# A long-convolution spectrum made one feed ahead, its halves moved by DMA, and eleven zero products at the start

## The chip, the core and the metric

The kernel runs on one core of a Trainium2 chip. The core has a matrix engine (TensorE, in the profile PE, its weight loads PEld), VectorE (DVE), ScalarE (ACT), GpSimd (POOL) and a queue engine, SyncE (SP), that only issues transfers; ACT and POOL can issue transfers too. Each engine works through its own instructions in a fixed order and waits on semaphores for the others. Working data lie in SBUF, 128 partitions wide; matmuls write to PSUM, in banks of 512 words per partition. The metric is the device time of one execution in microseconds (us), the median of several runs. Before the change it is 1204.5 us.

## The reference

Two kinds of layer alternate, A, B, A, B, over `x` of shape 2048 x 576, each behind a layer norm and added to its input:

```python
# A: Fourier mixing, both transforms as given matrices
a = x @ hid_re.T;  b = x @ hid_im.T
y = seq_re @ a - seq_im @ b
# B: gate, with a long causal convolution that does not depend on x
k_shift = causal_conv4(k, shift_k);  kv = k_shift * v
y = irfft(rfft(pad(kv)) * rfft(pad(ssm_k)))[:2048] + kv * ssm_D
out = q * y            # q is the normed x
```

The arguments `k`, `v`, `shift_k`, `ssm_k` and `ssm_D` are the same in both B layers, so the long convolution is made once. All is in float32. A float32 matmul is made of three in a rounded 32-bit format: high part by high part, high by low, low by high; that is why operands are "split" (ScalarE copies the rounded high part, VectorE subtracts to get the low part) and why matmuls come in threes.

## The kernel before

The first A layer's product with the sequence matrix runs in `layer` (line 291): four blocks of 512 output rows, two matrices (`g`), 16 steps of 128 rows each. One step is 14 matmuls of 512 columns (12 into four accumulators `s0` to `s3`, 2 into `rm`), with one 128 x 512 piece of the matrix, loaded by SP and split by `load_c` two steps ahead. In the first block each step also needs its normed block of `x` (`get_x0`, `to_x`). After each block the product with the hidden matrix (`hidden`, line 267) follows in pieces of 27 matmuls of 288 columns.

Beside it runs `branch` (line 338), a generator that makes the long convolution and is advanced between half steps of the layer. Its transforms of 4096 points are split as 128 by 16 and have three parts: first 128-point products (`f1_products`, stored to DRAM as `t`), the 16-point stage, and the last 128-point products (`i2_products`). The 16-point stage handles 64 "feeds" (`mids`: two halves of 288 channels times 32 groups of four frequencies). A feed is a 128 x 576 slice, loaded by SP (`load_feed`) and split (`split_feed`): its first 288 columns carry the signal, the next the convolution kernel. Partitions 0 to 63 (`lo`) end up with real parts, 64 to 127 (`hi`) with imaginary parts. For each feed the stage does this:

- `mid_inverse` of an older product: three matmuls, a copy out of PSUM by ACT, a store.
- `mid_kernel`: three matmuls give the kernel's spectrum in a PSUM bank; four ACT copies place it in `kk`, a buffer of two 288-column planes: plane 0 gets the real part in both halves, plane 1 the imaginary part in both halves, the lower one negated. There are two `kk` buffers.
- `mid_round`: the product of the feed before is split into `yf` for its inverse.
- `mid_signal`: three matmuls give the signal's spectrum; VectorE multiplies it with plane 0 (in place in `kk`), then each half with the other half of plane 1 into `p2`, and adds.
- the split of the feed two further on and the load of the one four further on.

The order in time comes from three things. The generator yields the planned cost of what it just issued (0.4, 1.6, 1.1 per feed; `I2_COST` for `i2_products`), and the loop over the layer's steps (line 752) advances it until the sum of these costs reaches what is due. A scheduler at build time then fixes each engine's order, roughly the written order where operands are expected in time. The helper `act` chains the branch's ACT instructions, so that these stay as written. All the narrow products, of the stage, of `hidden` and of `i2_products`, share three PSUM banks (`bank`, line 76).

At the start TensorE has nothing to do until the first loads have landed and been split.

Of the kernel before, what the change touches and what calls it, by code (L numbers as in the profile page):

```python
# [10 lines left out]
F32 = mybir.dt.float32  # L11
FR = mybir.dt.float32r
AF = mybir.ActivationFunctionType
OP = mybir.AluOpType

P = 128
S = 2048
D = 576
J = S // P
TB = 4  # L20
NT = 512
HD = D // 2
# [22 lines left out]
I2_COST = 2.0  # L45
# [13 lines left out]
SC_AT = 8 + 4 * STAT  # L59
RT_AT = SC_AT + 4 * REM + 5 * WIDE  # L60
FLT = RT_AT + NT


@with_exitstack
def fnet_h3_kernel(ctx: ExitStack, tc: tile.TileContext, x, c_mat, w_re, w_im, k_pad, v, shift_k,
                   ssm_k, ssm_d, f1c, i2c, midc, out):
    nc = tc.nc
# [5 lines left out]
    def mm(ps, lhsT, rhs, first, last, more=False):  # L73
        nc.tensor.matmul(ps, lhsT, rhs, start=first, stop=last, skip_group_check=more)  # L74
# [4 lines left out]
    acc4 = [psp.tile([P, NT], F32, tag=f"s{i}", name=f"s{i}") for i in range(4)]  # L79
# [25 lines left out]
    def flat(words, dt, name):  # L105
        return sb.tile([P, words], dt, tag=name, name=name)
# [29 lines left out]
    def two(v):  # L136
        return v.rearrange("p (a n) -> p a n", a=2)

    mats = flat(X_END + 3 * WIDE, FR, "mats")
    xs = mats[:, :X_END].rearrange("p (j n) -> p j n", j=J)  # L140
# [7 lines left out]

    flts = flat(FLT, F32, "flts")
    mhalf = flts[:, :1]  # L150
# [13 lines left out]

    nc.vector.memset(mhalf, -0.5)
    nc.scalar.activation(flts[:, 1:2], mhalf, AF.Copy)

    def norm_stats(src):
        m = ring["stat"]()
        st, mv, ve, rs = m[:, :12].rearrange("p (a c) -> p a c", a=2), m[:, 12:14], m[:, 14:15], m[:, 15:16]  # L170
        for i in range(2):
            nc.vector.bn_stats(st[:, i, :], src[:, i * HD:(i + 1) * HD])
        nc.vector.bn_aggr(mv, st)
        nc.vector.tensor_scalar(ve, mv[:, 1:2], EPS, None, op0=OP.add)  # L174
        pows.append(nc.gpsimd.tensor_tensor(rs, ve, mhalf, OP.pow).ins)  # L175
        return mv, rs, m[:, 16:17]
# [161 lines left out]
    def branch():  # L338
# [132 lines left out]
        lo, hi = slice(0, 64), slice(64, 128)  # L471

        def mid_half(df, o):
            ps = bank()
            mm(ps[:, :HD], mc[:, 0, :], df[0][:, o:o + HD], True, False)
            mm(ps[:, :HD], mc[:, 0, :], df[1][:, o:o + HD], False, False)
            mm(ps[:, :HD], mc[:, 1, :], df[0][:, o:o + HD], False, True)
            return ps
# [3 lines left out]
        def act(*args, **kw):  # L482
            if last_act:
                with tc.issue_after(last_act[-1]):
                    last_act.append(nc.scalar.activation(*args, **kw).ins)  # L485
            else:
                last_act.append(nc.scalar.activation(*args, **kw).ins)
# [4 lines left out]

        def mid_kernel(df):
            pk, kk = mid_half(df, HD), two(ring["kk"]())
            act(kk[:, 0, :], pk[:, :HD], AF.Copy)
            act(kk[lo, 1, :], kk[hi, 0, :], AF.Copy)
            act(kk[hi, 1, :], kk[hi, 0, :], AF.Copy, scale=-1.0)
            act(kk[hi, 0, :], kk[lo, 0, :], AF.Copy)
            return kk

        def mid_signal(df, kk):
            px = mid_half(df, 0)
            p1, p2 = kk[:, 0, :], ring["p2"]()
            nc.vector.tensor_tensor(p1, px[:, :HD], p1, OP.mult)
            nc.vector.tensor_tensor(p2[lo], px[hi, :HD], kk[hi, 1, :], OP.mult)
            nc.vector.tensor_tensor(p2[hi], px[lo, :HD], kk[lo, 1, :], OP.mult)
            nc.vector.tensor_tensor(p1, p1, p2, OP.add)
            return p1

        def mid_round(p1):  # L510
            yf = two(ring["yf"]())
            act_split(yf[:, 0, :], yf[:, 1, :], p1)
            return yf

        def mid_inverse(hf, qg, yf):
            pv = bank()
            mm(pv[:, :HD], mc[:, 2, :], yf[:, 0, :], True, False)
            mm(pv[:, :HD], mc[:, 2, :], yf[:, 1, :], False, False)
            mm(pv[:, :HD], mc[:, 3, :], yf[:, 0, :], False, True)
            vo = ring["vo"]()  # L520
            act(vo, pv[:, :HD], AF.Copy)
            nc.scalar.dma_start(v_d[hf][4 * qg:4 * qg + 4].rearrange("q j c d -> (q j c) d"), vo)

        def i2_products(hf, j, fc, vf):
            yo = ring["vo"]()
            ps = bank()
            for c in range(2):
                cs = slice(c * HD, (c + 1) * HD)
                mm(ps[:, :HD], fc[:, c, :], vf[0][:, cs], c == 0, False)
                mm(ps[:, :HD], fc[:, c, :], vf[1][:, cs], False, False)  # L530
                mm(ps[:, :HD], fc[:, 2 + c, :], vf[0][:, cs], False, c == 1)
            act(yo, ps[:, :HD], AF.Copy)
            nc.scalar.dma_start(yb_d[j][:, hf * HD:(hf + 1) * HD], yo)
# [3 lines left out]
        feeds = []  # L537
# [7 lines left out]
        landed, halves, fcs, yfs = {}, {}, {}, []  # L545
# [8 lines left out]
        def load_fc(k):  # L554
            if k < len(rows):
                fcs[k] = quads(ring["fc"]())
                load_fr(fcs[k], i2c[rows[k]])
# [9 lines left out]
        for i in range(2):  # L567
            split_feed(i)
            load_feed(i + 2)
            load_fc(i)  # L570
        used, ahead, product = 0, 2, None
        for i, (kind, hf, q) in enumerate(feeds):
            df = halves.pop(i)
            if kind:
                i2_products(hf, q, fcs.pop(used), df)
                load_fc(used + ahead)
                used += 1
            else:
                if len(yfs) == MID_LAG:
                    mid_inverse(*yfs.pop(0))  # L580
                    yield 0.4
                kk = mid_kernel(df)
                if product is not None:
                    yfs.append((*product[:2], mid_round(product[2])))
                yield 1.6
                product = hf, q, mid_signal(df, kk)
            split_feed(i + 2)
            load_feed(i + ahead + 2)
            if i == last_mid:
                yield 0.4  # L590
                mid_inverse(*yfs.pop(0))
                yfs.append((*product[:2], mid_round(product[2])))
                while yfs:
                    yield 0.4
                    mid_inverse(*yfs.pop(0))
                for name, t, at, words in (("fc", m1, spare, 4 * P), ("land", flts, kk_at, D)):
                    old = ring[name]
                    held = [old.tiles[(old.n + m) % 2] for m in range(2)]
                    fresh(name)
                    lay(t, at, (name, words, 2))  # L600
                    ring[name].tiles.extend(held)
                for m in range(2):
                    load_fc(used + ahead + m)
                    load_feed(i + ahead + 3 + m)
                ahead = 4
            yield I2_COST if kind else 1.1

    def sums(src, junk):
        m = ring["stat"]()
# [111 lines left out]
    used = 4  # L721
# [382 lines left out]
```

## Time and profile before

| what | value |
|---|---|
| median of 3 runs | 1204.5 us (1203.71 to 1204.72) |
| the profiled execution | 1203.45 us |
| its span, first to last instruction | 1201.7 us |
| TensorE busy | 1181.4 us (98%) |
| VectorE busy | 839.9 us (70%) |
| ScalarE busy | 666.0 us (55%) |
| moved by DMA | 261.95 MB, mean 218 GB/s |

Matmuls are pipelined and overlap, and the profile models their ends, so TensorE's 98% says that it is seldom empty, not that it works at its full rate; the distance from one start to the next tells that. A row of a group gives busy time, mean duration of one instruction, and the idle time of the engine just before such instructions with what ended most of it. A row of a stage gives its times and the busy time of each engine in it.

### The profile page before, as it was taken

To read this page: it belongs to the slowest core of one execution; us is meant where nothing else is said; L and a number is where in the kernel's file an instruction comes from. 1 tells how busy PE (TensorE), PEld (TensorE's weight loads), DVE (VectorE), ACT (ScalarE), POOL (GpSimd) and SP (SyncE) were. 2 spreads that over 40 slices of the span, in tenths; PEclk is the share of its full clock that TensorE was granted. 3 is DMA by queue.
4 is the path that set the end of the run, shared out by engine and by line. 5 is a ranking of instruction groups with operands and counts; after the bars stand their busy time and mean duration, and the time that the engine had idled before them with its cause. 6 is when DMAs were issued, how large, how long until landed. Compare 5 with 4: busy or idle time off the path is not lost.

```text
span 1201.7 us, 18251 instructions
## 1 busy us (share of the span) xinstructions
PE 1181.4 (98%) x6320; PEld 1026.7 (85%) x6320; DVE 839.9 (70%) x1498; ACT 666.0 (55%) x1335; POOL 75.3 (6%) x116
## 2 busy tenths in 40 slices
PE   7999999999999999999999999999999999999997
PEld 6888888988888888888988898888888888789997
DVE  7889983679777677675447766865776777674764
ACT  7865665679877768675435666534444445450210
POOL 2210000000000000001101121000000000001111
PEclk9999999999999999999999999999999999999999
DMA  9879898546756767648967686872772786795621
GB/s 355 273 242 310 282 296 262 177 133 182 217 183 194 212 178 207 194 143 247 308 202 237 221 257 204 278 259 71 225 274 71 216 283 213 270 339 155 218 92 40
DMA packets 146110, 261.95 MB, mean 218 GB/s; under 512 B 15841, under 2 KB 44769, under 8 KB 146018
## 3 DMA queue, kind: packets, MB, share of 16 engines
q1 hardware_dynamic: 102674, 205.58, 53.5%
q10 hardware_dynamic: 36432, 42.63, 10.2%
q0 software_dynamic: 6912, 12.59, 3.9%
q8 instruction: 49, 0.80, 0.3%
q14 instruction: 43, 0.35, 0.1%
HBM read 194.09 MB, written 66.65 MB: 217 GB/s over the span
## 4 chain that ended last, share of the span: by engine, by line
PE 84%; DVE 5%; ACT 4%; DMA 4%; issue 2%; POOL 1%; SPq 0%; ACTq 0%; POOLq 0%; DVEq 0%
PE s L74 46%; PE bk L74 33%; PE rm L74 5%; ACT flts L485 1%; DMA flts<-in_c_mat 1%; DVE mats L189 1%; DMA t<-ud 1%; DVE mats L92 1%; DVE f1f L386 1%; DMA t<-flts 1%; ACT mid L485 1%; ACT mats L91 1%; POOL flts L615 0%; DVE f1f L381 0%; DMA flts<-in_ssm_k 0%
## 5 line engine op out<-in xcount | busy, mean ns | idle before, releaser
L74 PE MATMUL s<-mats 128*128 128x512 f32 x2088 | 531.4, 392 | 1.3 <-DVE u L92 0.8
L74 PEld LDWEIGHTS s<-mats 128*128 128x128 f32 x2088 | 381.7, 188 | 71.9 <-DVE u L92 1.7
L92 DVE TENSOR_TENSOR mats<-flts,mats 128x512 fp32r<-128x512 f32 x206 | 141.1, 687 | 60.9 <-ACT mats L91 57.8
L91 ACT ACTIVATE mats<-flts 128x512 fp32r<-128x512 f32 x206 | 128.6, 628 | 81.8 <-PE bk L74 33.8
L74 PE MATMUL bk<-mid 128*128 128x288 f32 x768 | 131.2, 300 | 1.7 <-ACT flts L485 0.9
L74 PEld LDWEIGHTS bk<-mid 128*128 128x128 f32 x768 | 114.3, 188 | 21.3 <-ACT flts L485 8.4
L491 DVE TENSOR_TENSOR mid<-flts,mid 128x576 fp32r<-128x576 f32 (+1 forms) x160 | 101.9, 637 | 33.6 <-ACT mid L485 28.0
L74 PE MATMUL bk<-w,u 128*128 128x288 f32 x864 | 120.8, 296 | 0.4 <-DVE w L232 0.4
L74 PEld LDWEIGHTS bk<-w,u 128*128 128x128 f32 x864 | 117.3, 188 | 4.1 <-ACT flts L485 1.3
L485 ACT ACTIVATE flts<-bk 128x288 f32<-128x288 f32 x160 | 62.0, 405 | 86.8 <-PE bk L74 73.9
L74 PE MATMUL rm<-mats 128*128 128x512 f32 x304 | 94.9, 391 | 0.0
L485 ACT ACTIVATE mid<-flts 128x576 fp32r<-128x576 f32 (+1 forms) x159 | 86.7, 582 | 7.3 <-DMA flts<-t 3.3
L485 ACT ACTIVATE flts<-flts 64x288 f32<-64x288 f32 x192 | 85.0, 443 | 5.9 <-ACT flts L485 0.4
L431 ACT ACTIVATE flts<-bk 128x288 f32<-128x288 f32 x128 | 49.2, 409 | 47.1 <-PE bk L74 40.0
L74 PE MATMUL bk<-f1r 128*128 128x288 f32 x384 | 64.9, 301 | 7.2 <-ACT f1r L91 7.2
L74 PEld LDWEIGHTS bk<-f1r 128*128 128x128 f32 x384 | 59.8, 192 | 14.2 <-ACT f1r L91 7.6
L74 PE MATMUL bk<-mats 128*128 128x288 f32 (+1 forms) x376 | 67.8, 317 | 0.0
L74 PEld LDWEIGHTS rm<-mats 128*128 128x128 f32 x304 | 56.9, 188 | 12.1 <-DVE flts L264 0.3
L74 PE MATMUL s<-t,mats 128*128 128x512 f32 x264 | 65.5, 390 | 1.6 <-DVE t L92 1.6
L278 DVE TENSOR_TENSOR flts<-flts,bk 128x288 f32<-128x288 f32 x48 | 21.8, 453 | 63.2 <-PE bk L74 61.0
L175 POOL TENSOR_TENSOR flts<-flts 128x1 f32<-128x1 f32 x35 | 29.6, 846 | 526.0 <-DVE flts L174 522.6
L74 PEld LDWEIGHTS s<-t,mats 128*128 128x128 f32 x264 | 49.5, 188 | 12.2 <-DVE t L92 2.0
(143 smaller groups left out, 1500.7 us busy)
## 6 DMA issues: line engine op xcount, KB each, us to landing
flts<-in_c_mat SPq DMA_DIRECT2D x148, 256.0 KB, 3.7
ph<-in_c_mat SPq DMA_DIRECT2D x54, 512.0 KB, 4.4
t<-flts ACTq DMA_DIRECT2D x64, 288.0 KB, 4.5
flts<-t SPq DMA_DIRECT2D x64, 288.0 KB, 2.9
flts<-in_c_mat SPq DMA_DIRECT2D x30, 512.0 KB, 5.0
vd<-flts ACTq DMA_DIRECT2D x64, 144.0 KB, 2.3
flts<-vd SPq DMA_DIRECT2D x32, 288.0 KB, 4.9
mid<-in_i2c POOLq DMA_DIRECT2D x32, 256.0 KB, 5.6
```

Of the source, the lines that this page charges most:

```text
L74: nc.tensor.matmul(ps, lhsT, rhs, start=first, stop=last, skip_group_check=more)
L91: a = nc.scalar.activation(h, src, AF.Copy).ins
L92: return a, nc.vector.tensor_tensor(l, src, h.bitcast(F32), OP.subtract).ins
L175: pows.append(nc.gpsimd.tensor_tensor(rs, ve, mhalf, OP.pow).ins)
L189: made.append(nc.vector.tensor_tensor(t[:, D + REM:], y[:, :NC * P], h[:, :NC * P], OP.subtract).ins)
L278: added[:] = [nc.vector.tensor_tensor(r[:, cs], r[:, cs], ps[:, :HD], OP.add).ins]
L386: nc.vector.tensor_tensor(rp, rp, out_t, OP.add)
L431: stored[:] = [nc.scalar.activation(so[:, c, :], ps[:, :HD], AF.Copy).ins]
L485: last_act.append(nc.scalar.activation(*args, **kw).ins)
L491: nc.vector.tensor_tensor(l, src, h.bitcast(F32), OP.subtract)
```

## The change

Three things are edited. In `mid_kernel` ACT writes only two half copies out of PSUM, the real part to the lower and the imaginary part to the upper half of `kk`; two transfers issued by SP copy each to the other half. The negation moves from ACT's copy into one of VectorE's products, which becomes a `scalar_tensor_tensor` with a factor of -1. In the stage's loop the kernel spectrum of feed i + 1 is made within feed i, ahead of the signal products of feed i, and kept in `spectra`; the yields are cut anew to 0.4, 0.6, 0.5 and 1.6 (and 0.5 after an `i2_products` that is followed by a feed). At the start VectorE clears a part of the buffer `xs` that is not in use yet, and TensorE multiplies it with itself eleven times into `s0` to `s3`, which the layer's first step clears again.

```diff
+WARM = 11
@@ start
     nc.vector.memset(mhalf, -0.5)
     nc.scalar.activation(flts[:, 1:2], mhalf, AF.Copy)
+    warm = xs[:, J - 1, :NT + P]
+    nc.vector.memset(warm.bitcast(F32), 0.0)
+    for i in range(WARM):
+        mm(acc4[i % 4], warm[:, NT:], warm[:, :NT], True, True)
@@ branch
         def mid_kernel(df):
             pk, kk = mid_half(df, HD), two(ring["kk"]())
-            act(kk[:, 0, :], pk[:, :HD], AF.Copy)
-            act(kk[lo, 1, :], kk[hi, 0, :], AF.Copy)
-            act(kk[hi, 1, :], kk[hi, 0, :], AF.Copy, scale=-1.0)
-            act(kk[hi, 0, :], kk[lo, 0, :], AF.Copy)
+            act(kk[lo, 0, :], pk[lo, :HD], AF.Copy)
+            act(kk[hi, 1, :], pk[hi, :HD], AF.Copy)
+            nc.sync.dma_start(kk[hi, 0, :], kk[lo, 0, :])
+            nc.sync.dma_start(kk[lo, 1, :], kk[hi, 1, :])
             return kk
 
         def mid_signal(df, kk):
             px = mid_half(df, 0)
             p1, p2 = kk[:, 0, :], ring["p2"]()
             nc.vector.tensor_tensor(p1, px[:, :HD], p1, OP.mult)
-            nc.vector.tensor_tensor(p2[lo], px[hi, :HD], kk[hi, 1, :], OP.mult)
+            nc.vector.scalar_tensor_tensor(p2[lo], px[hi, :HD], -1.0, kk[hi, 1, :], op0=OP.mult, op1=OP.mult)
             nc.vector.tensor_tensor(p2[hi], px[lo, :HD], kk[lo, 1, :], OP.mult)
             nc.vector.tensor_tensor(p1, p1, p2, OP.add)
             return p1
@@ the stage's loop
-        used, ahead, product = 0, 2, None
+        used, ahead, product, spectra = 0, 2, None, {}
+
+        def kernel_ahead(i):
+            if i < len(feeds) and not feeds[i][0]:
+                spectra[i] = mid_kernel(halves[i])
+                return True
+
+        kernel_ahead(0)
         for i, (kind, hf, q) in enumerate(feeds):
             df = halves.pop(i)
             if kind:
                 i2_products(hf, q, fcs.pop(used), df)
                 load_fc(used + ahead)
                 used += 1
+                if kernel_ahead(i + 1):
+                    yield 0.5
             else:
                 if len(yfs) == MID_LAG:
                     mid_inverse(*yfs.pop(0))
                     yield 0.4
-                kk = mid_kernel(df)
                 if product is not None:
                     yfs.append((*product[:2], mid_round(product[2])))
-                yield 1.6
-                product = hf, q, mid_signal(df, kk)
+                yield 0.6
+                if kernel_ahead(i + 1):
+                    yield 0.5
+                product = hf, q, mid_signal(df, spectra.pop(i))
             split_feed(i + 2)
             load_feed(i + ahead + 2)
...
-            yield I2_COST if kind else 1.1
+            yield I2_COST if kind else 1.6
```

## The prediction

> **What bounds the kernel now.** I read the engine totals first, then the chain that ended last, then the 16-point stage by windows and by weight loads, because a busy TensorE in this profile isn't yet a TensorE at its rate.
>
> ```profile
> span 1201.7 us, 18251 instructions
> ...
> PE 1181.4 (98%) x6320; PEld 1026.7 (85%) x6320; DVE 839.9 (70%) x1498; ACT 666.0 (55%) x1335; POOL 75.3 (6%) x116
> ```
>
> The profiled execution took 1203.45 us, its span plus 1.75 us around it; the median of the runs is 1204.5, which is 1.05 more. The sum below is made against 1203.45. TensorE is the bound, so time is won or lost only where its matmuls stand further apart than they must. Their dense spacing comes from the chain in order of time:
>
> ```profile
> 654.75 2.72 PE s L74 x12
> 657.47 0.45 PE rm L74 x2
> 657.92 2.72 PE s L74 x12
> ...
> 1078.97 115.02 PE bk L74 x866
> ```
>
> From 654.75 to 657.92 lie 14 matmuls of 512 columns: 0.2264 us each. The last 866 of 288 columns take 115.02 us: 0.1328 each. The 16-point stage fills about 220 to 550 us. Its row for all engines, and its row for the tile bk alone, which holds the narrow matmuls (columns of the first: time, then busy us and count of PE, PEld, DVE, ACT, POOL, the granted clock, the busy share of the DMA engines and GB/s):
>
> ```profile
> 220.00:550.00 330.00, 327.92 (x1852) 285.47 (x1852) 247.23 (x485) 249.27 (x543) 5.30 (x10) 1.00 0.61 182
> ...
> 220.00:550.00 330.00, 168.96 (x1087) 1.00 0.61 182
> ```
>
> Of 1852 matmuls 1087 are narrow and 765 wide: 765 x 0.2264 + 1087 x 0.1328 = 173.2 + 144.4 = 317.6 us. So of 330 us TensorE loses 12.4 at full clock; that is all the stage can give. Who makes it wait is seen at the weight loads of the narrow matmuls in this window:
>
> ```profile
> L74 PEld LDWEIGHTS bk<-mid 128*128 128x128 f32 x628 | 93.8, 188 | 18.9 <-ACT flts L485 8.4 <-DVE flts L506 2.6 <-DVE mid L491 0.7
> L74 PEld LDWEIGHTS bk<-w,u 128*128 128x128 f32 x459 | 62.0, 188 | 2.1 <-ACT flts L485 1.1 <-DVE flts L506 0.4
> ```
>
> 9.5 us end with an ACT copy out of a PSUM bank (L485, flts<-bk) and 3.0 us with L506, the last of VectorE's reads of a signal's bank: TensorE waits for one of three banks to come free.
>
> **Part 1, ScalarE's copies.** Per kernel spectrum the change drops three ACT copies between halves of `kk` and splits the copy out of PSUM into two of 64 partitions.
>
> ```profile
> L485 ACT ACTIVATE flts<-flts 64x288 f32<-64x288 f32 x192 | 85.0, 443 | 5.9 <-ACT flts L485 0.4
> L485 ACT ACTIVATE flts<-bk 128x288 f32<-128x288 f32 x136 | 52.2, 404 | 55.4 <-PE bk L74 47.0 <-ACT flts L485 5.5 <-DVE mid L491 1.3
> ```
>
> Removed: 192 x 0.443 = 85.0 us. Added: one more PSUM copy for each of 64 spectra; as long per partition, so 0.404 each, 25.9 us (at most 0.443, the 64-partition row: 28.4). ACT's work in the stage falls from 249.3 to 190.2 us, 76% to 58%. A dense feed (14 wide and 9 narrow matmuls) lasts 3.17 + 1.20 = 4.37 us, and ACT gives back 0.92 of it. ACT runs this branch in written order, so the copy that frees a bank has been standing behind 1.33 us of SBUF copies. Ends: nothing (the free time lies elsewhere) and all 9.5. I take two thirds, -6.3, because the removed work stands just ahead of the late copies; a third stays for copies late behind other work (splits, rounding).
>
> **Part 2, VectorE no longer waits for the spectrum.**
>
> ```profile
> L504 DVE TENSOR_TENSOR flts<-bk,flts 128x288 f32<-128x288 f32 x64 | 29.1, 455 | 37.1 <-ACT flts L485 36.6
> ```
>
> Today the first product of a signal waits 36.6 us in all for the copies, holding the signal's bank. With the spectrum made one feed ahead it should be there. Of the 3.0 us charged to L506 I take half, -1.5 (ends 0 and -3.0). `scalar_tensor_tensor` in place of `tensor_tensor` for one product:
>
> ```profile
> L627 DVE SCALAR_TENSOR_TENSOR flts<-flts 128x576 f32<-128x576 f32 x10 | 8.1, 809 | 0.0
> ```
>
> 809 ns against 0.76 us for the two-operand form at 576 columns (L491 in the next fence) is 7%: 0.03 x 64 = 2 us on a VectorE that is 75% busy and loses 36.6 us of waiting. Cost nothing; without that cover, at most 2.
>
> **Part 3, the two transfers, and the new waits.** A spectrum now needs two SP transfers of 64 x 288, and the product for one feed must be rounded before the spectrum two feeds later may overwrite its `kk` (two of them, and the product is made in place). That is a loop over two feeds: ACT copies, transfer, products, sum, rounding, next copies. VectorE's part today:
>
> ```profile
> 307.29 0.46 DVE L504 TENSOR_TENSOR flts<-bk,flts 128x288 f32<-128x288 f32 x1 [1.23 <-ACT flts L485]
> 307.75 0.46 DVE L491 TENSOR_TENSOR mid<-flts,mid 128x288 fp32r<-128x288 f32 x1
> 308.25 0.46 DVE L505 TENSOR_TENSOR flts<-bk,flts 64x288 f32<-64x288 f32 x1
> 308.72 0.45 DVE L506 TENSOR_TENSOR flts<-bk,flts 64x288 f32<-64x288 f32 x1
> 309.20 0.76 DVE L491 TENSOR_TENSOR mid<-flts,mid 128x576 fp32r<-128x576 f32 x1
> 309.88 0.45 DVE L507 TENSOR_TENSOR flts<-flts 128x288 f32<-128x288 f32 x1
> ```
>
> First product to end of sum: 3.04 us (307.29 to 310.33), other work in between included. Two ACT copies 0.81; rounding, high part on ACT 0.44 (as long as the 64-partition copy), low part on VectorE 0.46. Together 4.75, plus the transfer from issue to landing. No row shows SBUF to SBUF; the nearest in this window:
>
> ```profile
> flts<-t SPq DMA_DIRECT2D x54, 288.0 KB, 2.9
> flts<-in_c_mat SPq DMA_DIRECT2D x54, 256.0 KB, 3.1
> vd<-flts ACTq DMA_DIRECT2D x57, 144.0 KB, 2.3
> wd<-w SPq DMA_DIRECT2D x9, 576.0 KB, 4.6
> ```
>
> The nearest is `vd`, also out of SBUF, in rows of 288 words: 2.3 us; each new transfer has half its bytes. The far end is 4.6. At 2.3 the loop takes 7.1 us against 2 x 4.37 = 8.74: it fits with 1.7 to spare, and over the stage's mean feed (330/64 = 5.16 us) with 3.3. By the last row a transfer that queues behind a big one takes the loop to 9.4.
>
> The Trainium skill, "DMA: Bandwidth & Descriptors", section "Queues, rings and completion order", says that SP's transfers share one ring on each DMA engine and are taken in ring order. By that rule a small copy issued behind a matrix load waits for its bytes, as the last case supposes; no row here shows such a pair.
>
> On SP, 128 issues are added, and behind each that still waits for ACT stand the feed loads, the matrix loads and, here and there, `wd` stores; ACT's splits wait for the loads. The code issues them two feeds and two row blocks ahead, 8.7 us at the dense rate against landings of 2.9 to 3.1, so a delay of a microsecond or two is covered. The spectrum's matmuls also move one feed up: they need the split of their feed sooner, and the two ACT copies wait in ACT's queue for VectorE's rounding, with the split and the next bank's copy behind them. I charge these new waits +3.0 together: 0.05 us a feed, a third of what ACT's late copies cost today (9.5/64 = 0.15). The planner's costs don't add to it: 0.4 + 0.6 + 0.5 + 1.6 a feed against 0.4 + 1.6 + 1.1, both 3.1; POOL's loads keep their place. Ends: 0, and 64 feeds x (9.35/2 - 4.37) = +20.
>
> **Part 4, the zero products.** They start once VectorE has cleared the operand, in time that TensorE spends waiting for its first load:
>
> ```profile
> 0.81 0.06 DVE L165 MEMSET flts<- 128x1 f32 x1 [0.81 <-PEq L1096]
> ...
> 6.96 2.60 PE L74 MATMUL bk<-f1r 128*128 128x288 f32 x9 [6.96 <-ACT f1r L91]
> 9.37 2.07 PE L74 MATMUL s<-mats 128*128 128x512 f32 x4
> ...
> 15.25 2.90 PE L74 MATMUL s<-mats 128*128 128x512 f32 x12
> ...
> 18.57 2.91 PE L74 MATMUL s<-mats 128*128 128x512 f32 x12
> ```
>
> The first nine narrow matmuls take 2.41 us, 0.268 each, half the dense rate. From 9.37 to 15.25 stand 14 wide and 6 narrow ones, 3.97 us of work in 5.88. So 1.2 + 1.9 = 3.1 us go to the slow start. Eleven wide zero products at half rate take 11 x 0.45 = 5.0 us; clearing 640 columns takes VectorE, after its first clearing, some 0.85 (0.76 for 576, above), so they start at about 1.75 and end by 6.75, ahead of 6.96: no delay. Were the clearing slower, TensorE would start later by what is over 0.2 us. But TensorE, once fast, meets its data:
>
> ```profile
> 12.00:16.00 4.00, 4.00 (x18) 3.28 (x18) 4.00 (x14) 3.71 (x7) 2.37 (x4) 1.00 1.05 389
> ...
> 14.04 0.67 ACT L186 ACTIVATE mats<-early 128x576 fp32r<-128x576 f32 x1
> ...
> 18.03 0.68 DVE L189 TENSOR_TENSOR mats<-early,mats 128x512 fp32r<-128x512 f32 x1
> ```
>
> The second row block is rounded at 14.71 and needed at 15.25: 0.54 us to gain. The third's low part is ready at 18.71 and used by the fifth matmul from 18.57, at 19.48: 0.77. VectorE, which makes these parts, has no idle time to give here (its row, third column of pairs, is 4.00 of 4.00 us), so I take -0.5; ends 0 and -3.1.
>
> The Trainium skill, "TensorE: Matmul & The Clock Gate", Part 1 on the HAM clock gate, gives half rate until one free-running window of about 3.4 us has been busy. By it 5 us of zeros hold a whole window in about half of all starts, (5.0 - 3.4)/3.4, and the term is -0.5 or 0; the trace agrees on the half rate (0.268 against 0.133), and no run here shows the phase.
>
> Sum: -6.3 - 1.5 + 3.0 - 0.5 = -5.3 us: 1198.2 for such an execution, 1199.2 beside the median.
>
> **Rivals.** (a) The transfer loop becomes the bound. For it: the loop is closed over only two buffers, DMA engines are 61% busy in the stage, and a landing of 4.6 us has a row. Against: the nearest rows have 2.3 to 3.1. It eats the gains (-8.3 with the start) when 64 x ((4.75 + L)/2 - 4.37) exceeds them, from L = 4.25 us; at 4.6 it costs 20 us, 1204.5 + 20 - 8.3 = 1216. Just past the point it gives 1207. (b) It is hidden anyway: the bank that ACT frees sooner waits for another reader, the zeros meet data that isn't there, new waits equal old ones: 1203.5. For it: VectorE is as busy as ACT and takes over. (c) Everything that ACT holds back comes, with no new wait: 9.5 and 0.8 at the start: 1204.5 - 10.3 = 1194.2. The other 12.4 - 9.5 = 2.9 belong to waits that part 1 doesn't touch. (d) The zeros give their whole 3.1 as well as the main case: 1196.6; against it stand the two gaps of 0.54 and 0.77.
>
> **How the numbers follow.** A change under 0.2% (2.4 us) can't be told from none. Main case 0.47 (its own range 1195.5 to 1202), (c) and (d) together 0.11, (b) 0.18, (a) 0.24. Faster 0.58, same 0.18, slower 0.24. The range leaves out the far half of (a) and of (c): 1194.5 to 1208.
>
> **What would show it.** Right: in the stage ACT busy falls to about 190 us, L504's wait for ACT is gone, the weight-load idle ended by L485 shrinks to about 3; the new SP transfers land in 2 to 3 us. Wrong: L504 waiting for a DMA, ACT waiting for the rounding (L491) with banks held behind it, or narrow weight loads ended by L491; at the start, the second block's matmul still near 15.2.

## The result, and the profile after

The changed kernel takes 1215.11 us (median; 1211.93 to 1216.98) beside 1204.11 for the kernel before on the same chip: ratio 1.0091, interval 1.0076 to 1.0106, so 11.0 us slower. The profiled execution took 1216.98 us, 13.5 more than the one of before; the reading below is against that.

The totals of the page after:

```profile
span 1215.1 us, 18579 instructions
...
PE 1188.9 (98%) x6331; PEld 1029.1 (85%) x6331; DVE 841.8 (69%) x1499; ACT 616.0 (51%) x1207; POOL 75.3 (6%) x116
```

ScalarE lost 50 us of work, as meant. The 16-point stage by windows, all engines and then the tile bk alone (columns as in the prediction):

```profile
220.00:550.00 330.00, 319.41 (x1774) 275.63 (x1774) 238.88 (x468) 192.42 (x400) 5.30 (x10) 0.99 0.70 203
...
220.00:550.00 330.00, 165.06 (x1036) 149.53 (x1036) 90.41 (x199) 78.81 (x193) 0.99 0.70 203
```

In the same 330 us TensorE started 1774 matmuls, not 1852. By the prediction's sum, 738 wide and 1036 narrow ones are 304.7 us of work: 25.3 us are lost where 12.4 were. These 12.9 are nearly the whole 13.5; some 1.7 of them lie in one stretch of 3.41 us at half clock (last section). The weight loads of the narrow matmuls in this window, and the waits of ScalarE and of VectorE (waiting line, line waited for, us, times, longest); L490 is before's L485, L496 its L491, L509 its L504, L512 its L507:

```profile
L75 PEld LDWEIGHTS bk<-mid 128*128 128x128 f32 x604 | 91.1, 188 | 30.4 <-DVE mid L496 8.7 <-ACT mid L490 8.5 <-ACT flts L490 3.5
```

```profile
ACT flts L490 <- DVE mid L496: 18.9, 29, 1.3
ACT mid L490 <- DVE flts L512: 18.7, 20, 4.6
```

```profile
DVE mid L496 <- ACT mid L490: 31.4, 39, 2.8
...
DVE flts L509 <- DMA flts<-flts: 9.8, 8, 5.3
```

The first row is the result in short. What ScalarE's copies out of the banks (flts L490) held back fell from 8.4 to 3.5 us, but two waits that were under 1 us now end 17.2: TensorE waits for the two parts of a feed's split (mid L490, ScalarE's high part; mid L496, VectorE's low part). And ScalarE's copies into `kk` wait 29 times for VectorE's rounding of a product, which they did not do before.

The stage's first microseconds show the whole chain. ScalarE's rows of the timeline after, then VectorE's, then TensorE's (start, us, then in brackets the idle time and who ended it):

```profile
221.22 1.70 ACT L490 ACTIVATE flts<-bk 64x288 f32<-64x288 f32 x4 [2.74 <-PE bk L75]
...
229.55 0.45 ACT L490 ACTIVATE mid<-flts 128x288 fp32r<-128x288 f32 x1 [4.63 <-DVE flts L512]
...
230.91 0.41 ACT L490 ACTIVATE flts<-bk 64x288 f32<-64x288 f32 x1 [0.92 <-DVE mid L496]
231.86 0.41 ACT L490 ACTIVATE flts<-bk 64x288 f32<-64x288 f32 x1
232.29 1.02 ACT L490 ACTIVATE mid<-flts 128x576 fp32r<-128x576 f32 x2
```

```profile
226.52 0.46 DVE L509 TENSOR_TENSOR flts<-bk,flts 128x288 f32<-128x288 f32 x1 [5.25 <-DMA flts<-flts]
226.90 0.75 DVE L496 TENSOR_TENSOR mid<-flts,mid 128x576 fp32r<-128x576 f32 x1
...
229.02 0.45 DVE L512 TENSOR_TENSOR flts<-flts 128x288 f32<-128x288 f32 x1
...
230.36 0.46 DVE L496 TENSOR_TENSOR mid<-flts,mid 128x288 fp32r<-128x288 f32 x1
```

```profile
227.70 0.54 PE L75 MATMUL bk<-mid 128*128 128x288 f32 x2 [1.60 <-DVE mid L496]
...
233.03 0.40 PE L75 MATMUL bk<-mid 128*128 128x288 f32 x1 [2.08 <-ACT mid L490]
```

Read it from the top. ScalarE copies the first two spectra at 221.22. VectorE's first product waits 5.25 us for a transfer, and the low part of the next feed stands behind it, ready only at 227.65: TensorE waits 1.60. The sum ends at 229.47, ScalarE's rounding has waited 4.63 us for it, VectorE's part of the rounding ends at 230.82, and only then may ScalarE overwrite `kk` (230.91). The split of a feed stands behind that copy, starts at 232.29, and TensorE has waited 2.08 us for it. From 211 to 277 us the changed kernel starts 22 wide and 9 narrow matmuls fewer than before: 22 x 0.2264 + 9 x 0.1328 = 6.2 us.

```profile
211.00:277.00 66.00, 64.81 (x406) 57.94 (x406) 48.51 (x95) 47.39 (x100) 0.00 (x0) 1.00 0.50 154
...
211.00:277.00 66.00, 47.69 (x321) 43.86 (x321) 18.87 (x43) 8.49 (x22) 1.00 0.50 154
```

```profile
211.00:277.00 66.00, 60.32 (x375) 54.07 (x373) 44.72 (x88) 34.28 (x70) 0.00 (x0) 0.97 0.57 165
...
211.00:277.00 66.00, 47.53 (x312) 43.96 (x312) 18.57 (x41) 13.03 (x32) 0.97 0.57 165
```

(The first pair is before, the second after.) Further on the waits are mostly shorter, but they come back. ScalarE's rows, the copies for every second spectrum, then a product of VectorE and a group of matmuls of TensorE:

```profile
303.56 0.84 ACT L490 ACTIVATE flts<-bk 64x288 f32<-64x288 f32 x2
...
313.18 0.84 ACT L490 ACTIVATE flts<-bk 64x288 f32<-64x288 f32 x2 [0.58 <-DVE mid L496]
...
323.61 0.84 ACT L490 ACTIVATE flts<-bk 64x288 f32<-64x288 f32 x2 [0.59 <-DVE mid L496]
```

```profile
319.97 0.46 DVE L509 TENSOR_TENSOR flts<-bk,flts 128x288 f32<-128x288 f32 x1 [2.50 <-PE rm L75]
```

```profile
322.23 0.53 PE L75 MATMUL bk<-mid 128*128 128x288 f32 x2 [1.54 <-DVE mid L496]
```

From one filling of a buffer to the next pass 9.62 and 10.43 us, against 8.74 for two dense feeds. That alone shows little: the first products of every second feed start 10.4 us apart in the mean of the kernel before, too (10.7 after). The waits inside say more.

In the first round the transfers land within 2.5 us. VectorE starts the product 4.06 us after the copies have ended, and the sum ends 2.57 us later. ScalarE takes the rounding up only 1.13 us after that, because a split of the layer's matrix and a copy out of a bank stand ahead of it in its order. The rounding takes 0.93 us, and the next copies have waited 0.58 us for it.

In the second round the product at 319.97 waits 2.50 us. The profile names TensorE, but the product's transfer, issued at 313.61, landed 6.26 us later, at 319.88, the longest landing of all; the low part of a split stands behind that product, and TensorE waits 1.54 us.

By the landings in the trace eight more first products start 0.1 us after their transfer has landed; with this one they have waited 7.6 us, and with the 5.25 at the entry 12.9.

At the start, TensorE's rows after, then of before:

```profile
1.62 4.27 PE L75 MATMUL s<-mats 128*128 128x512 f32 x11 [1.62 <-DVE mats L169]
6.62 1.85 PE L75 MATMUL bk<-f1r 128*128 128x288 f32 x9 [0.73 <-ACT f1r L92]
...
13.86 3.17 PE L75 MATMUL s<-mats 128*128 128x512 f32 x12
...
29.99 1.46 PE L75 MATMUL bk<-f1r 128*128 128x288 f32 x9 [1.43 <-ACT flts L436]
...
35.01 1.29 PE L75 MATMUL s<-mats 128*128 128x512 f32 x5
```

```profile
34.35 1.98 PE L74 MATMUL s<-mats 128*128 128x512 f32 x8
```

The second row block starts at 13.86, not 15.25: 1.39 us won. At 29.99 TensorE waits for a copy out of a bank, and the matmul that before started at 34.35 now starts at 35.01. A lead of 0.38 us is there again from about 150 us on, up to the stage.

### The profile page after: what moved, and what is told of

Same layout as the page of the kernel before. It is cut to its first block, busy times and chain, and to the rows that moved or that the text cites. A ratio compares the mean times of both kernels' runs of the same rounds, so it can differ in the third digit from the quotient of the medians.

```text
span 1215.1 us, 18579 instructions
## 1 busy us (share of the span) xinstructions
PE 1188.9 (98%) x6331; PEld 1029.1 (85%) x6331; DVE 841.8 (69%) x1499; ACT 616.0 (51%) x1207; POOL 75.3 (6%) x116
## 4 chain that ended last, share of the span: by engine, by line
PE 81%; DMA 6%; DVE 5%; ACT 4%; issue 2%; POOL 0%; SPq 0%; ACTq 0%; POOLq 0%; DVEq 0%
PE s L75 45%; PE bk L75 32%; PE rm L75 4%; DMA flts<-in_c_mat 1%; DMA flts<-flts 1%; ACT mid L490 1%; DVE mid L496 1%; ACT flts L490 1%; DMA t<-flts 1%; DMA early<-in_x 1%; ACT mats L92 1%; DMA flts<-t 1%; DVE f1f L391 0%; DMA t<-ud 0%; DVE mats L194 0%
## 5 line engine op out<-in xcount | busy, mean ns | idle before, releaser
L490 ACT ACTIVATE flts<-bk 64x288 f32<-64x288 f32 (+1 forms) x224 | 91.5, 408 | 126.0 <-PE bk L75 88.4
L75 PE MATMUL bk<-mid 128*128 128x288 f32 x768 | 134.8, 302 | 10.3 <-DVE mid L496 5.5
L75 PEld LDWEIGHTS bk<-mid 128*128 128x128 f32 x768 | 115.1, 188 | 33.8 <-ACT mid L490 10.5
L496 DVE TENSOR_TENSOR mid<-flts,mid 128x576 fp32r<-128x576 f32 (+1 forms) x160 | 101.6, 637 | 58.9 <-ACT mid L490 50.4
L490 ACT ACTIVATE mid<-flts 128x576 fp32r<-128x576 f32 (+1 forms) x159 | 92.0, 585 | 25.2 <-DVE flts L512 19.5
L436 ACT ACTIVATE flts<-bk 128x288 f32<-128x288 f32 x128 | 49.4, 410 | 46.2 <-PE bk L75 43.8
L75 PE MATMUL bk<-mats,t 128*128 128x288 f32 (+1 forms) x368 | 59.3, 303 | 0.0
L75 PEld LDWEIGHTS bk<-mats 128*128 128x128 f32 x376 | 55.5, 188 | 3.4
```

The costliest lines, as they stand in the source:

```text
L436: stored[:] = [nc.scalar.activation(so[:, c, :], ps[:, :HD], AF.Copy).ins]
L496: nc.vector.tensor_tensor(l, src, h.bitcast(F32), OP.subtract)
```

## The experiments

Two theories stood at first. Order: the spectrum, made a feed ahead, needs its split a feed sooner, and its copies stand ahead of that split in ScalarE's order. Transfers: their landing holds VectorE's products. Ratios are to the kernel before on the same chip, with their intervals; the changed kernel's is 1.0091 (1.0076 to 1.0106).

**Each part alone.** The kernel before with nothing but the zero products:

```diff
+    warm = xs[:, J - 1, :NT + P]
+    nc.vector.memset(warm.bitcast(F32), 0.0)
+    for i in range(WARM):
+        mm(acc4[i % 4], warm[:, NT:], warm[:, :NT], True, True)
```

> The kernel before with the zero products alone. Both theories of the stage say nothing here. From the progress of the first layer's matmuls in the changed kernel (1.38 us ahead at the second row block, 0.38 ahead from about 130 us on) I expect 0.4 us less than before, between 0 and 0.8; if it were the whole slow start it would be 3.1 less.

1202.87 us, ratio 1.0001 (0.9989 to 1.0013): nothing. The changed kernel without these four lines:

> The changed kernel without the zero products. Both theories: the loss stays whole, 10.5 to 12 us over before; if the two edits disturbed each other it would be under 8.

1210.98 us, ratio 1.0064 (1.0045 to 1.0084): 8.0 us over before, less than the 10.5 to 12 expected, but not under 8. Most of the loss is the stage's; the interval just meets that of the whole change, so whether the zero products cost something there stays open.

**Order without transfers, twice.** First the changed kernel without its two transfers (`kk` is cleared once instead):

```diff
-            nc.sync.dma_start(kk[hi, 0, :], kk[lo, 0, :])
-            nc.sync.dma_start(kk[lo, 1, :], kk[hi, 1, :])
...
+        for _ in range(2):
+            nc.vector.memset(ring["kk"](), 0.0)
```

> The changed kernel without the two transfers, so the copied halves of the spectrum stay zero (they are cleared once, some 1.2 us of VectorE) and those products are left out of the result; ACT's load, the order and everything else stay. Order theory (the spectrum's matmuls come a feed sooner than the split that they need, which stands on ACT behind copies that wait for a rounding): still 7 to 11 us over before, weight loads still waiting for splits by some 13 us. Transfer theory (VectorE waits in its order for transfers that land in up to 6.3 us, and the low part of a split stands behind that wait): 0 to 5 us under before, weight loads waiting for splits under 4 us.

1208.43 us, ratio 1.0040 (1.0026 to 1.0053), in between: the order alone costs some 5 us, and the rest needs the transfers. ScalarE's wait for the rounding is untouched:

```profile
ACT flts L490 <- DVE mid L496: 22.6, 28, 4.1
```

Then the changed kernel with ScalarE's four copies of before in their place:

```diff
-            act(kk[lo, 0, :], pk[lo, :HD], AF.Copy)
-            act(kk[hi, 1, :], pk[hi, :HD], AF.Copy)
-            nc.sync.dma_start(kk[hi, 0, :], kk[lo, 0, :])
-            nc.sync.dma_start(kk[lo, 1, :], kk[hi, 1, :])
+            act(kk[:, 0, :], pk[:, :HD], AF.Copy)
+            act(kk[lo, 1, :], kk[hi, 0, :], AF.Copy)
+            act(kk[hi, 1, :], kk[hi, 0, :], AF.Copy, scale=-1.0)
+            act(kk[hi, 0, :], kk[lo, 0, :], AF.Copy)
```

> The changed kernel with its order and zero products, but ScalarE makes the four copies of before and no transfer is issued. Order theory: ScalarE is as busy as before (about 250 us in the stage) and its copies wait for the rounding as well, so the kernel takes 1212 to 1220. Transfer theory: without a landing the spectrum is in time, and it takes 1201 to 1206.

(The negated product is a `tensor_tensor` again in this run.) 1215.83 us, ratio 1.0112 (1.0095 to 1.0129): as slow as the whole change, with no transfer in it. The pure transfer theory falls. TensorE waits 20.7 us for splits, but only 2.8 for ScalarE's copies out of the banks, although ScalarE makes all four copies (243.96 us busy in the stage):

```profile
L75 PEld LDWEIGHTS bk<-mid 128*128 128x128 f32 x603 | 89.9, 188 | 31.2 <-ACT mid L490 14.6 <-DVE mid L496 6.1 <-ACT flts L490 2.8
```

**Transfers without the order.** The changed kernel with each spectrum just ahead of its own signal, as before:

```diff
-                yield 0.6
-                if kernel_ahead(i + 1):
-                    yield 0.5
-                product = hf, q, mid_signal(df, spectra.pop(i))
+                yield 1.6
+                product = hf, q, mid_signal(df, kk)
```

(with `kk = mid_kernel(df)` ahead of the rounding, and the last yield 1.1)

> The changed kernel with its transfers and zero products, but each spectrum is made just ahead of its own signal again, as before, with before's planner costs. Order theory (the loss comes from moving the spectrum ahead): the splits are in time again and the kernel takes 1203 to 1207. Transfer theory: nothing now lies between the copies and the product, so VectorE's first product waits some 2.8 us for a landing in nearly each of 64 feeds, over 100 us in all against 36.6 before, holds the signal's bank for it, and the kernel takes 1212 or more.

1218.31 us, ratio 1.0133 (1.0115 to 1.0152). The wait that the profile puts down to transfers is 16.4 us, not the 100 expected, but the banks are held: TensorE's weight loads wait 15.2 us for the third read of a signal's bank (L511). The pure order theory falls as well.

```profile
L509 DVE TENSOR_TENSOR flts<-bk,flts 128x288 f32<-128x288 f32 x61 | 27.7, 454 | 26.6 <-DMA flts<-flts 16.4 <-PE bk L75 5.5 <-PE rm L75 4.3
```

```profile
L75 PEld LDWEIGHTS bk<-mid 128*128 128x128 f32 x597 | 89.4, 188 | 33.2 <-DVE flts L511 15.2 <-ACT flts L490 9.7 <-DVE flts L283 1.3
```

**Another queue.** The transfers issued by GpSimd:

```diff
-            nc.sync.dma_start(kk[hi, 0, :], kk[lo, 0, :])
-            nc.sync.dma_start(kk[lo, 1, :], kk[hi, 1, :])
+            nc.gpsimd.dma_start(kk[hi, 0, :], kk[lo, 0, :])
+            nc.gpsimd.dma_start(kk[lo, 1, :], kk[hi, 1, :])
```

> The changed kernel with the two transfers issued by GpSimd, which has little to do, in place of SyncE. Queueing (a transfer behind SyncE's matrix loads and stores lands in up to 6.3 us, and SyncE's loads wait behind transfers that wait for ScalarE): the longest landing falls to about 3 us, VectorE's wait for transfers falls from 10 us to under 4, and the kernel takes 1208 to 1212. Order theory: the splits and the rounding are as late as they were, and it stays at 1212 to 1217. That GpSimd issues a transfer more slowly would add up to 1 us to each landing: 1217 or more.

1216.64 us, ratio 1.0115 (1.0099 to 1.0130). The median landing is the same in both queues, the longest is 5.3 us in place of 6.3, and VectorE's wait is no less; queueing in SP's own queue isn't what makes them late. What does stays open. (The changed kernel's DMA row, then this one's, then VectorE's waits here.)

```profile
flts<-flts SPq DMA_DIRECT2D x128, 72.0 KB, 2.8
```

```profile
flts<-flts POOLq DMA_DIRECT2D x128, 72.0 KB, 2.8
```

```profile
DVE flts L509 <- DMA flts<-flts: 11.3, 9, 5.8
```

**The split moved.** The changed kernel with the split at the head of a feed's body:

```diff
             df = halves.pop(i)
+            split_feed(i + 2)
...
-            split_feed(i + 2)
```

> The changed kernel with the split of feed i + 2 written at the head of the loop's body, ahead of the rounding, of the spectrum's copies and of the signal's products; its load stays where it was. Order theory: the waits of the spectrum's matmuls for a split (13.3 us in the stage) go almost whole, 1202 to 1206 us. Transfer theory: the low part now stands ahead of VectorE's wait, but the wait itself stays and holds the signal's bank: 1208 to 1213 us, with VectorE's first product still waiting for transfers by 10 us or more.

1210.08 us, ratio 1.0052 (1.0032 to 1.0071), where the transfer theory had put it; VectorE's first products wait 15.3 us for transfers, as it said. The waits for splits went, but ScalarE still waits for the rounding, and TensorE now waits 8.1 us, not 3.5, for the banks that ScalarE frees behind it. So neither the landing nor the wait for the rounding goes with the split:

```profile
ACT flts L490 <- DVE mid L496: 24.2, 34, 3.7
```

```profile
L75 PEld LDWEIGHTS bk<-mid 128*128 128x128 f32 x618 | 93.0, 189 | 19.0 <-ACT flts L490 8.1 <-DVE flts L511 3.5 <-DVE flts L283 0.8
```

**The rounding taken out of the loop.** A third theory, the loop: `kk` holds the product until it is rounded, and in the written order the rounding stands just ahead of the copies that reuse the buffer. With the sum written into `p2`, `kk` is free at the sum:

```diff
-            nc.vector.tensor_tensor(p1, p1, p2, OP.add)
-            return p1
+            nc.vector.tensor_tensor(p2, p1, p2, OP.add)
+            return p2
```

> The changed kernel, but the sum of a signal's two products is written into `p2` instead of into `kk`, so a spectrum's buffer is free at the sum and no longer at the rounding behind it. Loop theory (ScalarE's copies of the next spectrum wait for VectorE's rounding of a product, 23 us in the stage, and everything behind them in ScalarE's written order is late): that wait falls under 8 us, TensorE's waits for the splits of a feed fall from 13 us to under 6, and the kernel takes 1204 to 1208. Order theory (the splits are needed a feed sooner, whatever the copies wait for): the split waits stay at 10 us or more, and it takes 1211 to 1215. Transfer theory (the landing holds the signal's products): 1211 to 1215, with VectorE's first product still waiting for transfers some 10 us.

1206.03 us, ratio 1.0030 (1.0019 to 1.0041). In this kernel scratch of the layers, which shares `p2`'s words, overwrites some sums before they are rounded, so the next run is the one that counts. With `p2` at words of its own:

```diff
-("land", D, 2), ("kk", D, 2), ("vo", HD, 3), ("p2", HD, 1)
+("land", D, 2), ("kk", D, 2), ("vo", HD, 2), ("p2", HD, 1)
```

> As the run with the sum apart, with `p2` at words of its own: two buffers of `vo` instead of three make room (`p2` shared its words with scratch of the layers, which in the earlier run wrote over some sums between sum and rounding; the instructions and their sizes are the same). Loop theory: the same gain as there, 1203 to 1208, with ScalarE's copies no longer ended by VectorE's rounding. If that gain came only from sums that were overwritten and so not waited for, the time goes back to 1211 or more. If two buffers of `vo` are too few, ScalarE's copies show waits for the stores out of `vo` of over 5 us in the stage, and it takes 2 to 5 us more than 1206.

1204.83 us, ratio 1.0011 (1.0001 to 1.0020): 0.80% of 1203, 9.6 us, come back from one operand (and two `vo` buffers in place of three, to make room). Among ScalarE's waits of over 4 us none names the rounding any more, and TensorE's for the splits are 4.9 and 3.9 us:

```profile
L75 PEld LDWEIGHTS bk<-mid 128*128 128x128 f32 x630 | 95.2, 188 | 20.0 <-DVE mid L496 4.9 <-ACT mid L490 3.9 <-ACT flts L490 1.7
```

**Then the halves' copies.** The same with GpSimd copies in place of transfers:

```diff
-            nc.sync.dma_start(kk[hi, 0, :], kk[lo, 0, :])
-            nc.sync.dma_start(kk[lo, 1, :], kk[hi, 1, :])
+            nc.gpsimd.tensor_copy(kk[hi, 0, :], kk[lo, 0, :])
+            nc.gpsimd.tensor_copy(kk[lo, 1, :], kk[hi, 1, :])
```

> As the run with the sum apart and words of its own, and GpSimd copies the two halves inside the core in place of SyncE's transfers. Transfer theory (what is left of the loss is the landing of 2 to 6 us, at the stage's entry above all): VectorE's wait of 9.5 us for transfers goes, and the kernel takes 1198 to 1203. Order theory (what is left is the splits needed a feed sooner): it stays at 1204 to 1208. GpSimd's copies have no row here; were they 2 us or more each, they would land no sooner than the transfers and it would take 1205 or more.

1205.28 us, ratio 1.0013 (1.0003 to 1.0023): no gain, although VectorE's wait for the copies is 1.0 us. What is left there is the split, which the weight loads wait for as before (4.3 and 4.0 us):

```profile
L509 DVE TENSOR_TENSOR flts<-bk,flts 128x288 f32<-128x288 f32 x64 | 29.0, 453 | 4.5 <-PE bk L75 3.4 <-POOL flts L502 1.0
```

```profile
L75 PEld LDWEIGHTS bk<-mid 128*128 128x128 f32 x630 | 94.8, 188 | 19.7 <-DVE mid L496 4.3 <-ACT mid L490 4.0 <-DVE flts L511 2.3
```

With the split first as well (the diff of above):

> As the run before it in this call, with the split of the feed two ahead at the head of a feed's loop body instead of its end. Order theory: TensorE's 6 us of waits for splits go, and with the early release of the spectrum's buffer nothing takes their place: 1198 to 1203. Rival: the copies out of the banks now stand behind the split on ScalarE (0.68 us), the banks come free later, and it takes 1204 to 1209.

1199.56 us, ratio 0.9974 (0.9964 to 0.9985): faster than both kernels. The waits for splits are gone from the weight loads' row (its 0.6 us of mid L490 are the rounding of a product), and by the sum of above (770 wide, 1123 narrow) the stage loses 6.5 us of 330:

```profile
L75 PEld LDWEIGHTS bk<-mid 128*128 128x128 f32 x638 | 95.9, 188 | 13.2 <-ACT flts L490 3.6 <-DVE flts L511 1.3 <-ACT mid L490 0.6
```

```profile
220.00:550.00 330.00, 329.27 (x1893) 291.95 (x1892) 250.64 (x494) 199.40 (x420) 65.03 (x140) 1.00 0.64 189
...
220.00:550.00 330.00, 169.41 (x1123) 160.04 (x1124) 95.32 (x211) 81.79 (x202) 1.00 0.64 189
```

In this version the three ways to fill the halves can be compared. Transfers:

> The faster version (sum apart in words of its own, split first) with SyncE's two transfers in place of GpSimd's copies: the change with its order mended and its transfers kept. If the transfers cost next to nothing once the order leaves them a feed of time: 1198.5 to 1201.5. If their landing of 2 to 6 us is a cost of its own: 1203 to 1207, with VectorE's first product waiting 8 us or more for transfers.

1206.77 us, ratio 1.0037 (1.0023 to 1.0051): 0.63%, 7.6 us, more than GpSimd's copies, with the wait that was expected (VectorE's row for L509):

```profile
L509 DVE TENSOR_TENSOR flts<-bk,flts 128x288 f32<-128x288 f32 x62 | 28.1, 453 | 23.1 <-DMA flts<-flts 17.8 <-PE bk L75 3.2 <-PE rm L75 1.9
```

```profile
L75 PEld LDWEIGHTS bk<-mid 128*128 128x128 f32 x619 | 93.1, 189 | 18.3 <-ACT flts L490 5.0 <-DVE flts L511 4.8 <-DVE mid L496 2.0
```

The product that waits holds its signal's bank: TensorE waits 4.8 us in this row for the third read, 1.3 in the fast version. With transfers the earlier split even loses: the same kernel with the split last had 1.0011.

ScalarE's four copies:

> The faster version with ScalarE's four copies of before in place of GpSimd's. If ScalarE's 59 us are worth what the first part of the forecast said (6.3 us): 1204 to 1208. If they lie beside other work and only the order counts: 1199 to 1202.

1201.58 us, ratio 0.9987 (0.9973 to 1.0001). ScalarE is 252.5 us busy in the stage, not 199.4, and that is worth 0.13%, 1.6 us, which the intervals don't tell from none (3.7 at most). TensorE waits for ScalarE's bank copies no longer than in the fast version, 3.8 us against 3.6:

```profile
L75 PEld LDWEIGHTS bk<-mid 128*128 128x128 f32 x636 | 95.6, 188 | 13.9 <-ACT flts L490 3.8 <-ACT mid L490 1.5 <-DVE flts L511 1.2
```

The fast version without zero products:

> The faster version without the zero products. They were worth nothing in the kernel before (ratio 1.0001), so 1198.5 to 1200.5; if the half rate at the stage's entry swallowed their gain there, 0.5 to 1.5 more than with them.

1199.62 us, ratio 0.9969 (0.9958 to 0.9981): nothing again.

**The order of before with the same remedies.** The kernel before with the split first:

> The kernel before with the split of the feed two ahead at the head of a feed's loop body. If the faster version owes its gain to the earlier split alone: 1199 to 1201. If the split was not late in the kernel before (its waits for splits are 0.6 us in the stage), moving it ahead of the copies that free the banks costs: 1203 to 1207.

1204.91 us, ratio 1.0015 (1.0006 to 1.0024): there the split wasn't late, and it holds the copies back: weight loads wait 13.4 us for ScalarE's bank copies, 9.5 before. Before's order with GpSimd's copies:

> The kernel before's order (each spectrum just ahead of its own signal), with the two copies out of PSUM on ScalarE, the two copies between halves on GpSimd, and the zero products. If it is the landing that made the version with transfers in this order slow (1218), a copy of under 1 us inside the core takes it away: VectorE's wait for a spectrum falls to before's 37 us or less, ScalarE has 59 us less to do, and the kernel takes 1199 to 1203. If it is the order of the three reads of a signal's bank, or the GpSimd copy is slow (over 1.5 us), it takes 1206 or more.

1212.73 us, ratio 1.0085 (1.0071 to 1.0098). VectorE's wait for the copies is only 15.4 us, against 36.6 before, and yet TensorE's weight loads wait 13.5 us for the third read of a signal's bank (L511; 8.1 and 5.4 in the last two rows), as in the version with transfers in this order. VectorE's sum is slower too, 553 ns against 453 in the fast version. How much of the loss each makes wasn't told apart.

```profile
L512 DVE TENSOR_TENSOR flts<-flts 128x288 f32<-128x288 f32 x61 | 33.7, 553 | 0.1
L509 DVE TENSOR_TENSOR flts<-bk,flts 128x288 f32<-128x288 f32 x61 | 27.5, 451 | 16.3 <-POOL flts L502 15.4 <-PE bk L75 0.8
```

```profile
L75 PEld LDWEIGHTS bk<-mid 128*128 128x128 f32 x603 | 89.7, 188 | 22.6 <-DVE flts L511 8.1 <-ACT flts L490 6.1 <-DVE mid L496 1.5
L75 PEld LDWEIGHTS bk<-w,u 128*128 128x128 f32 x443 | 59.8, 188 | 9.5 <-DVE flts L511 5.4 <-ACT w L236 1.6 <-ACT flts L490 1.2
```

A third `kk` buffer, the plain way out of the loop, wasn't tried: `flts`, where these buffers lie, has no 576 words left. Nor was the earlier split with GpSimd's copies alone, without the sum apart.

## Why the prediction was wrong

**Part 1** had the wait nearly right and its reason wrong. ScalarE's busy time in the stage is 192.4 us (190.2 forecast), and TensorE's wait for its bank copies fell from 9.5 to 3.8 us in the rows of `mid` and `w,u`, 5.7 of the 6.3 forecast. But the removed copies are not why. With all four copies in the changed order this wait is 3.1 us. With two copies in the order of before it is 10.7 (transfers) and 7.3 (GpSimd), and another reader of the same banks, VectorE's third read, ends 16.4 and 13.5 us. So the short wait goes with the spectrum's earlier place, not with ScalarE's load. Once nothing else held the stage up, ScalarE's four copies cost 1.6 us more than GpSimd's two, which the intervals don't tell from none; they exclude 6.3. A share of waits ended by an engine isn't the time that comes back when that engine has less to do.

**Part 2** held in part: the first product no longer waits for ScalarE, and the `scalar_tensor_tensor` takes 0.46 us, as long as the product that it replaces. But the product now waits for transfers, 12.9 us in place of 36.6, and TensorE's waits for the third read of a bank, of which 1.5 were to go, are 3.2 us where they were 3.0.

**Part 3** is the step that failed: "I charge these new waits +3.0 together". The weight-load idle that the splits end alone is 17.2 us, from 0.7 in the row of before. Two of its judgements were wrong.
The first is "it fits with 1.7 to spare". The loop was summed as if its members followed one another at once, 7.1 us. In the two rounds shown they don't: 1.13 us pass before ScalarE takes the rounding up in one, and a landing takes 6.26 us in the other. What closes the loop is the written order: in each feed `mid_round` stands directly ahead of the copies that reuse its buffer, and the split for two feeds on directly behind them, so sum, rounding on two engines, copies, split on two engines and the next matmuls form one chain through each feed. I had named "the split and the next bank's copy behind them" and then priced it by a share of ScalarE's old waits, which has nothing to do with that chain. Freeing `kk` at the sum gave 9.6 us back; with the split first and the transfers gone, 14.1 us (1.0091 to 0.9974, times 1203).
The second is the landing, taken as 2.3 us in each feed. Its median is 2.8, but 12 of the 115 landings that the trace has take over 4.25 us, the point from which by the prediction it decides. Leaving the transfers out of the changed kernel gave 6.1 us back (1.0091 to 1.0040). This doesn't add to the 9.6: with the sum apart, GpSimd's copies gain nothing more (1.0011 against 1.0013), as it should be if landing and rounding are members of one loop, which a buffer freed sooner opens. With the split first the landing costs 7.6 us again, at the signal's bank; why the earlier split makes it matter stays open.

The cited ring rule (the Trainium skill, "DMA: Bandwidth & Descriptors", section "Queues, rings and completion order") was no guide to the loss: the landing by GpSimd's queue has the same median, 2.8 us, and a wait as long, 5.8. The landing of 6.26 us is a case as it supposes, issued by SP 0.65 us behind a `wd` store and 1.03 behind a matrix load; but by GpSimd's queue landings also reach 5.3 us.

**Part 4** was right in its mechanism: the zero products start at 1.62 us (1.75 forecast), and the second row block comes 1.39 sooner, more than the 0.54 of its gap, since its rounding, taken as fixed at 14.71, ends at 13.81. But most of the lead is lost by 35 us, at a bank that ScalarE frees late. Two runs, on the kernel before and on the fast version, measure no gain; the first excludes more than 1.3 us, so the slow start's 3.1 don't come back, while 0.5 can't be told from none.

**The rivals.** (a), "the transfer loop becomes the bound", was the outcome, and its 1207 to 1216 holds 1215.1; it had 0.24, and the range cut off its far half. That its far end comes so near is luck: 1216 stands for 4.6 us in every feed. Its condition was on the landing alone, and it left the rounding's place in the written order out. Of the prediction's own signs of being wrong three came: the first product waits for a transfer, ScalarE waits for the rounding, and splits end narrow weight loads. But its signs of being right came too (ScalarE at 192 us, no wait of the product for ScalarE, 3.8 us, a median landing of 2.8), so these could not tell the two outcomes apart.

## What to carry to other kernels

Before moving a step a stage ahead, write down, for each buffer that it fills, which instruction frees it, and where that instruction stands in the written order of the engine that waits: a loop that fits in its summed durations need not fit if its last member is issued just ahead of its first, and a median landing hides the long ones. An in-place result keeps an input's buffer for the whole life of the result; here one output operand was worth 9.6 us. And before pricing a wait by the engine that ends it, ask whether the new order moves that wait anyway. When an edit with a sound idea loses, look at what the new order makes late: here a loss of 0.9% became a gain of 0.3% with the sum's operand, the split's place and the engine of two copies changed.

## What the runs showed of the hardware

TensorE's clock falls to half for one window without a long pause. Windows of the changed kernel at the stage's entry (granted clock after the counts):

```profile
230.14:233.55 3.41, 1.32 (x8) 0.86 (x7) 2.79 (x6) 2.35 (x5) 0.00 (x0) 1.00 0.45 114
233.55:236.96 3.41, 3.41 (x17) 3.41 (x16) 0.58 (x2) 1.50 (x3) 0.00 (x0) 0.50 0.71 223
```

In the 3.41 us ahead of it TensorE was busy 1.32 us, and its longest wait was 2.08. So short stalls can cost twice: half of this window's work, some 1.7 us (an estimate, half of 3.41), is lost on top of them. The Trainium skill, "TensorE: Matmul & The Clock Gate", Part 1 on the HAM clock gate, gives the half rate after at least one idle window of about 3.4 us; the window's length agrees with the trace, but this one was not idle. The profile of before has no such window in the stage. Behind the start and ahead of the end, eight such windows stand in seven of the 18 profiles, one of them in the kernel before with the zero products (220.44 us). In the 3.41 us ahead of each TensorE was busy 23 to 59%; but two stretches of 49 and 52% (the changed kernel with each spectrum just ahead of its signal, and the changed kernel, both at 479 us) had no half clock behind them, so the share alone doesn't decide.

In the kernel with before's order and GpSimd's copies, the 28 sums (L512) of the stage's window that overlap a GpSimd copy take 671 ns in the mean, the 33 others 452, by the start and end of each in the trace. The Trainium skill, "GPSIMD Engine Reference", section "1. Specifications", says that GpSimd's SBUF interfaces are contended by VectorE's instructions with two SBUF inputs; these sums have two. One of the 28 takes 451 ns, and in the fast version the only sum that overlaps a copy takes 457, so not every overlap costs.
